# Where the routed experts' second layer and read-outs stand around eight runtime switches

## The chip, the cores and the metric

The kernel runs on one core of a Trainium2 chip. The metric is the device time of one execution in microseconds. The engines are PE (TensorE, matrix products), ACT (ScalarE), DVE (VectorE), POOL (GpSimd) and SP (SyncE, which issues most of the transfers). Each runs its own list of instructions in order, and they meet through semaphores. Where a branch depends on data, every engine takes it for itself.

## The reference

Three stages follow one another: a retention attention, a dense layer with a rational activation, and a mixture of experts. The change lies in the third:

```python
logits = x @ w_gate + modality_bias[modality_id]
e_idx = np.argmax(logits, axis=1)
...
for e in range(E):                       # 8 experts
    mask = e_idx == e
    if not mask.any():
        continue
    h = np.maximum(x[mask] @ w1[e], 0.0)         # 512 -> 1024
    out[mask] = gate_w[mask, None] * (h @ w2[e]) # 1024 -> 512
```

There are 3072 tokens. How many go to an expert is known only when the kernel runs.

## The kernel before

Values are split into a high and a low float16 part, and each product is made of three matmuls. Tokens are first written, sorted by expert, to a buffer `xs` in memory. Then the experts follow one another, `e` = 0 to 7.

Each expert has a static part of 288 columns (tokens) and an extra part of n columns, n = 0, 32, ..., 224. The static part is in the program as it stands. The extra part lies in one of the eight arms of a `tc.Switch` (L867), and each engine jumps to the arm that the count selects. `switch_hint` (L847) tells each engine the arm ahead of the jump, once the count has been loaded (`values_load`, L830). With these inputs the arms taken are n = 0, 128, 128, 192, 32, 64, 160 and 192 for the eight experts. A last `tc.If(redo > 0)` (L885) holds the path for an expert with more than 512 tokens; it is not taken here.

- `hidden` (matmuls L504) makes 128 of the 1024 hidden values of the columns: 12 matmuls, then a relu on ACT (L525, L535) and the low part on POOL or DVE (L537). Eight such steps, f0 to f7, make the layer; their results are `ht`. For extra columns `hidden_tile` does the same (`hq`, `hf`, `hx`).
- `combine` is the second layer: for the 288 columns, two tiles of 128 rows (L592) and one of 32 rows (L599), in three PSUM banks `acc0`, `acc1`, `acc2`, tile by tile within each f. Extra columns use `acc3`, `m`, `r`.
- `emit` is the read-out of a tile: for 128 rows a scale on DVE (L607), for the small ones a copy on ACT (L609), three additions (L611) and a scale (L612) on DVE; then an indirect transfer to `out`, issued by POOL (L613).
- Weights come in 512 KB pieces into five staging buffers (L439, L443 on SP), and `digest` splits each on ACT (L455) and DVE (L456). An expert has eight pieces. `weights()` fetches ahead and digests one; calls of it (`cfill`) stand between the steps of the layers.

The order is written out by hand: each engine does things in the order of the code. Expert 0 and 1 have an early part: the first 192 columns of expert 0's hidden layer and all 288 of expert 1's are made before the counts are known. Then stand the count (L772), two digests, and the loop. For each e: the count is read, the hint given, the hidden steps made that are left (`hd`; for e of 2 and above f3 to f7, since f0 to f2 stand in the arm before), with the read-outs of the expert before among them (the list `late`), then the static second layer, then the switch. An arm holds the extra hidden columns, the steps f0 to f2 of the next expert, and the extra second layer with its read-outs. The last expert has its static second layer and read-outs inside the arms, between its extra hidden columns and their second layer.

Of the kernel before, what the change touches and what calls it, by code (L numbers as in the profile page):

```python
# [54 lines left out]
def retention_moe_kernel(ctx, tc, qkv, qk, kv, w_in, w_out, ma, mb, mod, wg, mbias, w1, w2, consts, ids, out, dbg=None):  # L55
# [451 lines left out]
    def cut(n):  # L507
        tiles = [(t * P, P) for t in range(n // P)]
        for m in (64, 32):
            if n & m:  # L510
                tiles.append((sum(t[1] for t in tiles), m))
        return tiles
# [59 lines left out]
            ht.append(h)  # L572
        return lambda f: ht[f // m][:, f % m]

    def combine(nm, v2, ht, n, tags, fillers=(), serial=False):
        fillers = list(fillers)
        tiles = cut(n)
        spots = {}
        for a, b, h, l in places(n):
            for lo in range(a, b, P):  # L580
                spots[lo] = lo + h - a, lo + l - a
        ac = [ps.tile([P, DM], F32, tag=tag, name=f"ya{nm}_{lo}", bufs=1) for tag, (lo, _) in zip(tags, tiles)]
# [196 lines left out]
    def early(e, f):  # L779
        hidden(e, f, wts[e, 0], xge, 0, EARLY[e], "he", col[e], dve if (e, f) > (1, 0) else pool)  # L780
# [23 lines left out]
    early(0, 7)  # L804
    rank1()
    early(1, 0)
    mt, xg = load_rows("0", xs[:512], 512, EARLY[0])
    mtn, xgn = load_rows("1", xs[REG : REG + 512], 512, EARLY[1])
    for f in range(1, KF2):
# [13 lines left out]
    )  # L823
    dve.tensor_reduce(cnx[:, :E], over, axis=AX.X, op=ALU.add)
    dve.tensor_copy(cni[:, 2 * E + 1 :], cnx[:, :E])
    weights(2)

    def grains(e):
        at = 2 * E + 1 + e
# [3 lines left out]
        return nc.values_load(cni[0:1, e : e + 1], min_val=-NTOK if e == 2 * E else 0, max_val=NTOK)  # L833

    late = []

    for e in range(E):
# [8 lines left out]
        sel = grains(e)  # L846
        tc.switch_hint({g: sel for g in mybir.ALL_ENGINES}, nthr + 1, label=f"x{e}")  # L847
        lo = EARLY[e] if e < 2 else 0
        for f in range(FILL if e > 1 else 0, KF2):
            if lo < BASE:  # L850
                hidden(e, f, wts[e, 0], xg, lo, BASE, "hd")
            if late:
                late.pop(0)()
            if e > 1 and f in HFILL:
                cfill()
        def whole(nm):
            ac = combine(nm, wts[e, 1], lambda f, e=e: hts[e, f][:, 0], BASE, ("acc0", "acc1", "acc2"), [cfill if f < CFILL[min(e, 2)] else lambda: None for f in range(KF2)])
            return [lambda e=e, mt=mt, a=a, lo=lo, n=n: emit(e, nm, a, mt, SLOT[lo][1], n) for a, (lo, n) in ac]

        if last:  # L860
            redo = count(2 * E)
        else:
            late.extend(whole(e))
            if e:
                for f in range(FILL):
                    hidden_home(e + 1, f)
        for n in tc.Switch(sel, nthr + 1, hint=f"x{e}"):  # L867
            nm = f"{e}x{n}"
            n *= GRAIN
            if n:  # L870
                ht = hidden_tile(nm, wts[e, 0], xg, BASE, n, dve)
            if last:
                for f in whole(f"{e}b{n}"):
                    f()
            elif e:
                for f in range(FILL):
                    hidden(e + 1, f, wts[e + 1, 0], xgn, 0, BASE, f"hd{n}f", wide=False)
            if n:
                ac = combine(nm, wts[e, 1], ht, n, ("acc3", "m", "r"), serial=last)
                for a, (lo, m) in reversed(ac):  # L880
                    emit(e, nm, a, mt, SLOT[BASE + lo][1], m)
        if not last:
            mt, xg = mtn, xgn

    with tc.If(redo > 0):  # L885
        for e in range(E):
            cnt, start = count(e), count(E + e)
            with tc.If(cnt > start):
# [92 lines left out]
```

## Time and profile before

| | |
|---|---|
| median of 3 runs | 1014.28 us (1014.16 to 1014.75) |
| the profiled execution: its time | 1011.81 us |
| the profiled execution: its span | 1010.0 us |
| PE busy | 920.8 us, 91% of the span |
| DVE, ACT, POOL busy | 658.2, 603.7, 527.9 us |
| DMA, mean over the span | 119 GB/s |

The span is the part of the profiled execution in which engines worked. The experts take the stretch from about 660 us to the end. The timeline gives an instruction group's start and duration and, in brackets, how long its engine had been idle before it and what ended that. The waits sum this idle time by what ended it. `PEldq`, `POOLq` and the like are the engines' sequencers, which take branches and semaphores.

### The profile page before, as it was taken

To read this page: it belongs to the slowest core of one execution; us is meant where nothing else is said; L and a number is where in the kernel's file an instruction comes from. 1 tells how busy PE (TensorE), PEld (TensorE's weight loads), DVE (VectorE), ACT (ScalarE), POOL (GpSimd) and SP (SyncE) were. 2 spreads that over 40 slices of the span, in tenths; PEclk is the share of its full clock that TensorE was granted. 3 is DMA by queue.
4 is the path that set the end of the run, shared out by engine and by line. 5 is a ranking of instruction groups with operands and counts; after the bars stand their busy time and mean duration, and the time that the engine had idled before them with its cause. 6 is when DMAs were issued, how large, how long until landed. Compare 5 with 4: busy or idle time off the path is not lost.

```text
span 1010.0 us, 16225 instructions
## 1 busy us (share of the span) xinstructions
PE 920.8 (91%) x5957; PEld 503.0 (50%) x5957; DVE 658.2 (65%) x973; ACT 603.7 (60%) x964; POOL 527.9 (52%) x519
## 2 busy tenths in 40 slices
PE   8877889999999999989999999997799999999973
PEld 6534445444555445545444444455355664555641
DVE  4798777787888788877686797875426244553221
ACT  0376656877777677766776886874335454554320
POOL 2687878646666646666545545542315334344221
PEclk8779989999999999999999999998899999999987
DMA  8654877252214121410051033225665554672001
GB/s 280 197 208 143 262 223 251 86 153 93 67 63 126 73 77 61 105 43 1 1 146 43 1 80 105 85 63 164 173 203 162 171 163 146 178 209 60 15 26 43
DMA packets 105786, 119.93 MB, mean 119 GB/s; under 512 B 72030, under 2 KB 72286, under 8 KB 105568
## 3 DMA queue, kind: packets, MB, share of 16 engines
q1 hardware_dynamic: 101504, 104.98, 34.8%
q0 software_dynamic: 4064, 12.64, 3.5%
q8 instruction: 65, 1.06, 0.5%
q14 instruction: 153, 1.25, 0.4%
HBM read 81.83 MB, written 21.35 MB: 102 GB/s over the span
## 4 chain that ended last, share of the span: by engine, by line
PE 48%; DVE 17%; DMA 10%; issue 9%; POOL 8%; ACT 6%; SPq 0%; POOLq 0%; ACTq 0%; DVEq 0%; another core or an unknown queue 0%
PE hp L299 13%; PE acc L351 13%; PE ya L592 6%; DMA out<-yo2x,mt 5%; DMA out<-yo,mt 4%; PE y L231 2%; POOL q L310 2%; POOL xs L418 2%; PE sc L212 2%; PE y L229 2%; DVE q L321 2%; DVE r L320 2%; DVE q L319 2%; DVE p L312 1%; POOL gt L340 1%
## 5 line engine op out<-in xcount | busy, mean ns | idle before, releaser
L351 PE MATMUL acc<-woh,gt 128*128 128x512 f16 x768 | 245.3, 381 | 0.3 <-POOL gt L340 0.3
L299 PE MATMUL hp<-xt,wih 128*128 128x512 f16 x768 | 232.5, 385 | 1.1 <-DVE p L313 1.0
L310 POOL TENSOR_TENSOR q<-q,a 128x512 f32<-128x512 f32 x96 | 133.7, 1393 | 183.5 <-ACT q L309 183.2
L351 PEld LDWEIGHTS <-gt 128*128 128x128 f16 x1152 | 110.4, 98 | 127.7 <-issue 4.0
L299 PE MATMUL hp<-xt,wil 128*128 128x512 f16 x384 | 147.1, 383 | 0.0
L351 PE MATMUL acc<-wol,gt 128*128 128x512 f16 x384 | 146.3, 381 | 0.0
L504 PEld LDWEIGHTS <-we 128*128 128x128 f16 x1536 | 119.3, 100 | 36.7 <-issue 18.6
L319 DVE SCALAR_TENSOR_TENSOR q<-q,r 128x512 f32<-128x512 f32 x96 | 65.6, 683 | 95.7 <-ACT r L327 95.4
L299 PEld LDWEIGHTS <-wih 128*128 128x128 f16 x768 | 74.0, 99 | 91.4 <-issue 7.4
L340 POOL TENSOR_TENSOR gt<-q,gt 128x512 f16<-128x512 f32 x95 | 111.3, 1172 | 0.0
L326 ACT ACTIVATE r<-q,one 128x512 f32<-128x512 f32 x96 | 65.7, 684 | 66.9 <-POOL q L310 66.9
L456 DVE SCALAR_TENSOR_TENSOR we<-sw,we 128x1024 f16<-128x1024 f32 x64 | 83.3, 1332 | 31.0 <-ACT we L455 30.8
L307 ACT ACTIVATE p<-hp,co 128x512 f32<-128x512 f32 x96 | 74.3, 774 | 29.2 <-PE hp L299 28.9
L592 PE MATMUL ya<-we,ht 128*128 128x512 f16 x336 | 82.1, 396 | 10.1 <-DVE we L456 7.3
L309 ACT ACTIVATE q<-a,co 128x512 f32<-128x512 f32 x96 | 78.1, 814 | 12.1 <-POOL gt L340 3.4
L312 DVE TENSOR_TENSOR p<-p,hp 128x512 f32<-128x512 f32 x96 | 65.2, 679 | 14.9 <-ACT a L308 14.9
L455 ACT ACTIVATE we<-sw 128x1024 f16<-128x1024 f32 x64 | 64.9, 1042 | 16.9 <-DMA sw<-in_w 16.8
L313 DVE SCALAR_TENSOR_TENSOR p<-p,co,hp 128x512 f32<-128x512 f32 x96 | 71.6, 746 | 2.9
L320 DVE SCALAR_TENSOR_TENSOR r<-p,co,r 128x512 f32<-128x512 f32 x96 | 71.7, 747 | 0.0
L537 POOL TENSOR_TENSOR ht<-hfhd,ht 128x256 f16<-128x256 f32 (+1 forms) x76 | 51.3, 706 | 38.9 <-ACT ht L535 20.9
L339 ACT ACTIVATE gt<-q 128x512 f16<-128x512 f32 x96 | 59.9, 624 | 15.8 <-DVE q L321 11.2
L321 DVE SCALAR_TENSOR_TENSOR q<-q,r 128x512 f32<-128x512 f32 x96 | 65.9, 687 | 3.3
(232 smaller groups left out, 1392.2 us busy)
## 6 DMA issues: line engine op xcount, KB each, us to landing
sw<-in_w SPq DMA_DIRECT2D x64, 512.0 KB, 4.6
qk<-in_qk SPq DMA_DIRECT2D x22, 512.0 KB, 3.5
xs<-zrow SPq DMA_DIRECT2D x8, 1032.0 KB, 8.9
spare<-in_moe_w_in SPq DMA_DIRECT2D x8, 1024.0 KB, 6.2
spare<-in_moe_w_out SPq DMA_DIRECT2D x8, 1024.0 KB, 5.0
qk<-in_qkv SPq DMA_DIRECT2D x13, 512.0 KB, 4.9
kv<-in_qkv SPq DMA_DIRECT2D x13, 512.0 KB, 6.1
kv<-in_kv SPq DMA_DIRECT2D x11, 512.0 KB, 4.7
```

The lines of the kernel that those rows point to most:

```text
L299: pe.matmul(hp, wi[wj][:, k, f * P : (f + 1) * P], xt[:, xj, k], start=n == 0, stop=n == 3 * KD - 1)
L309: act.activation(q, a, AF.Identity, scale=b1, bias=b0)
L310: pool.tensor_tensor(q, q, a, op=ALU.mult)
L312: lambda: dve.tensor_tensor(p_, p_, hp, op=ALU.mult),
L319: lambda: dve.scalar_tensor_tensor(q, q, 1.0 + 1e-6, r, op0=ALU.add, op1=ALU.mult),
L320: lambda: dve.scalar_tensor_tensor(r, p_, n0, r, op0=ALU.add, op1=ALU.mult),
L321: lambda: dve.scalar_tensor_tensor(q, q, 2.0, r, op0=ALU.subtract, op1=ALU.mult),
L340: (dve if i == NS - 1 else pool).tensor_tensor(gt[:, 1], g, gt[:, 0], op=ALU.subtract)
L351: pe.matmul(accs[s], gt[:, gj, s * P : (s + 1) * P], wo[wj][:, f], start=f == 0 and gj == 0 and wj == 0, stop=f == NF - 1 and gj == 1)
L456: dve.scalar_tensor_tensor(dl, sv, sc, dh, op0=ALU.mult, op1=ALU.subtract)
L504: pe.matmul(hp, v1[:, wj, k, f * P : (f + 1) * P], xg[:, xj, k, cols], start=c == 0, stop=c == 3 * KD - 1)
L592: pe.matmul(a, ht(f)[:, at : at + P], v2[:, wj, f], start=first and at == h and wj == 0, stop=last and at == l)
```

## The change

1. One more weight piece is fetched after the first early step of expert 1, and one digest instead of two stands after the count.
2. Expert 0: the first tile of its static second layer (columns 0 to 127) is made ahead of the hint and of the hidden steps that are left. The other two tiles go into the switch's arms; three digests and the three read-outs follow the switch.
3. Expert 1 takes the banks `acc3`, `m`, `r` for its static tiles and `acc2`, `acc0`, `acc1` for the extra ones.
4. The static read-outs of experts 1 to 6 move from the next expert's hidden steps into the arms of their own switch, one behind each of the three hidden steps there.
5. Last expert: the hidden steps f5 to f7 move into the arms, behind the extra hidden columns; the extra second layer and its read-outs stay in the arm, and the static second layer comes after the switch, tile by tile from the last (32 rows) to the first.
6. The overflow path is given `preferred_fallthrough_block=False`: its empty block now stands first, and the body behind it.

```diff
+    def combine(nm, v2, ht, n, tags, fillers=(), serial=False, pick=slice(None), ac=None):
...
+        tiles = cut(n)[pick]
...
     early(1, 0)
+    prefetch()
     mt, xg = load_rows("0", xs[:512], 512, EARLY[0])
...
-    weights(2)
+    weights()
...
+        tags = ("acc3", "m", "r") if e == 1 else ("acc0", "acc1", "acc2")
+        xtags = ("acc2", "acc0", "acc1") if e == 1 else ("acc3", "m", "r")
...
+        out0 = []
+        if e == 0:
+            out0 = base("0a", pick=slice(0, 1))
+        announce()
+        if e != 1:
+            lo = EARLY[e] if e == 0 else 0
+            for f in range(FILL if e else 0, KF2 - FILL if last else KF2):
                 hidden(e, f, wts[e, 0], xg, lo, BASE, "hd")
-            if late:
-                late.pop(0)()
...
         if last:
             redo = count(2 * E)
+            inner = [(e, f, wts[e, 0], xg) for f in range(KF2 - FILL, KF2)]
+        elif e:
+            out0 = base(e, fill=CFILL[min(e, 2)])
+            inner = [(e + 1, f, wts[e + 1, 0], xgn) for f in range(FILL)]
...
+        for n in tc.Switch(sel[e], nthr + 1, hint=f"x{e}"):
...
+            outs = list(out0)
             if n:
                 ht = hidden_tile(nm, wts[e, 0], xg, BASE, n, dve)
+            if e == 0:
+                late[:] = out0 + base(f"0b{n}", pick=slice(1, 3), ac=ac0)
+            for k in inner:
+                hidden(*k, 0, BASE, f"hd{n}f", wide=False)
+                if e and outs:
+                    outs.pop(0)()
             if n:
-                ac = combine(nm, wts[e, 1], ht, n, ("acc3", "m", "r"), serial=last)
+                ac = combine(nm, wts[e, 1], ht, n, xtags)
...
+        if e == 0:
+            weights(3)
+            for f in late:
+                f()
+        if last:
+            for f in reversed(base(e, serial=True)):
+                f()
...
-    with tc.If(redo > 0):
+    with tc.If(redo > 0, preferred_fallthrough_block=False):
```

Where the instructions stand: three places. Names carry the expert and the tile: `ya0_128` is expert 0's static tile from column 128, `hd0_0` its hidden step f0, `yo2x4_3` a read-out of expert 2's arm 4. `cni` holds the counts.

PE from the count to the first products of expert 1, before (the last early step is just ahead of it):

```order
L772 MATMUL cntp_6680<-cum24_6487,ones_356 128x8 [waits Activation_49]
L830 TENSOR_LOAD cni_5784 [waits DVE_49]
...
L847 BRANCH_PREFETCH_HINT
L504 LDWEIGHTS we0_0_5375
L504 MATMUL hd0_0_6755<-xg0_6523,we0_0_5375 128x96 [waits DMAHW3_49]
...
L599 MATMUL ya0_256_6901<-we0_1_6230,ht0_7_6482 32x512
...
L867 BRANCH_PREFETCH_HINT
L977 UNCONDITIONAL_BRANCH [waits PE_49]
...
L830 TENSOR_LOAD cni_5784
...
L592 LDWEIGHTS ht1_0_6517
L592 MATMUL ya1_0_8188<-we1_1_6694,ht1_0_6517 128x512 [waits DVE_49]
```

After:

```order
L773 MATMUL cntp_6680<-cum24_6487,ones_356 128x8 [waits Activation_49]
L593 LDWEIGHTS ht0_0_6246
L593 MATMUL ya0a_0_6697<-we0_1_6230,ht0_0_6246 128x512
...
L593 MATMUL ya0a_0_6697<-we0_1_6230,ht0_7_6482 128x512
L832 TENSOR_LOAD cni_5784 [waits DVE_49]
...
L858 BRANCH_PREFETCH_HINT
L504 LDWEIGHTS we0_0_5375
L504 MATMUL hd0_0_6776<-xg0_6525,we0_0_5375 128x96 [waits DMAHW4_49]
...
L882 BRANCH_PREFETCH_HINT
L593 LDWEIGHTS ht0_0_6246
L593 MATMUL ya0_1_6920<-we0_1_6230,ht0_0_6246 128x512
```

The count's load, and with it the hint, has moved behind the 24 matmuls of `ya0a`. The arm's entry hint now stands between the hidden steps and the tiles `ya0_1` and `ya0_2`, which are in every arm.

DVE at the switch of expert 2, arm 4 (128 extra columns, the one taken), before:

```order
L537 TENSOR_TENSOR hx2x4_10766<-hf2x4_1_10869,hx2x4_10766 128x4x128 [waits Activation_49]
L607 TENSOR_SCALAR yo2x4_3_10952<-ya2x4_0_10927,mt2_8108 128x512 [waits DMASW7_49,DMASW3_49,PE_49]
L977 UNCONDITIONAL_BRANCH
...
L830 TENSOR_LOAD cni_5784
...
L847 BRANCH_PREFETCH_HINT
L607 TENSOR_SCALAR yo2_0_11761<-ya2_0_10032,mt2_8108 128x512 [waits DMASW3_49,DVE_49,PE_49]
L456 SCALAR_TENSOR_TENSOR we4_0_10092<-sw4_1_10064,we4_0_10092 128x1024 [waits DMAHW7_49,Activation_49]
L607 TENSOR_SCALAR yo2_1_11789<-ya2_128_10033,mt2_8108 128x512 [waits DMASW1_49,DMASW5_49,DVE_49,PE_49]
L456 SCALAR_TENSOR_TENSOR we4_0_10092<-sw4_2_10080,we4_0_10092 128x1024 [waits DMAHW0_49,Activation_49]
L611 TENSOR_TENSOR yo2_2_11817<-yo2_2_11817,ya2_256_10034 32x512 [waits DMASW2_49,DMASW6_49,PE_49,Activation_49]
```

After, the whole of the arm (its first two rows are the low parts of the extra hidden columns):

```order
L537 TENSOR_TENSOR hx2x4_11246<-hf2x4_0_11296,hx2x4_11246 128x4x128 [waits DMASW5_49,PE_49,DMASW6_49,Activation_49,DMASW7_49,Pool_49]
L537 TENSOR_TENSOR hx2x4_11246<-hf2x4_1_11349,hx2x4_11246 128x4x128 [waits Activation_49]
L608 TENSOR_SCALAR yo2_0_11371<-ya2_0_10437,mt2_8398 128x512 [waits DMASW1_49,DMASW5_49,DVE_49,PE_49]
L608 TENSOR_SCALAR yo2_1_11394<-ya2_128_10438,mt2_8398 128x512 [waits DMASW0_49,PE_49]
L612 TENSOR_TENSOR yo2_2_11417<-yo2_2_11417,ya2_256_10439 32x512 [waits DMASW3_49,DMASW7_49,PE_49,Activation_49]
L612 TENSOR_TENSOR yo2_2_11417<-yo2_2_11417,ya2_256_10439 32x512 [waits DVE_49] x2
L613 TENSOR_SCALAR yo2_2_11417<-yo2_2_11417,mt2_8398 32x512 [waits DVE_49]
L608 TENSOR_SCALAR yo2x4_3_11451<-ya2x4_0_11426,mt2_8398 128x512 [waits DMASW6_49,DMASW2_49,PE_49]
L1001 UNCONDITIONAL_BRANCH
L882 BRANCH_PREFETCH_HINT
```

The five rows that read `ya2` (one of them is two instructions) have moved from behind the next expert's hint into the arm, ahead of the read-out of the extra tile.

POOL from the end of the last switch's arm 6 (192 extra columns) to the end of the program, before:

```order
L613 DMA out_0<-yo7x6_5_20700,mt7_17201 3072x512 [waits DMAHW3_49,DMASW5_49,DVE_49]
L613 DMA out_0<-yo7x6_3_20707,mt7_17201 3072x512 [waits DMAHW1_49,DMASW6_49,DVE_49]
L867 ISA [waits DMASW7_49]
L977 UNCONDITIONAL_BRANCH
...
L885 COMPARE_AND_BRANCH
...
L885 ISA [waits Pool_49,Pool_sequencer_49,DMASW4_49,DMASW5_49,DMASW3_49,DMASW6_49,DMASW2_49,DMASW7_49,DMASW1_49,DMASW0_49]
L885 UNCONDITIONAL_BRANCH
L977 ISA [waits barrier_Pool_Activation_PE_DVE_SP_gather]
```

After:

```order
L614 DMA out_0<-yo7x6_5_21500,mt7_18157 3072x512 [waits DMAHW1_49,DMASW2_49,DVE_49]
L614 DMA out_0<-yo7x6_3_21507,mt7_18157 3072x512 [waits DMAHW7_49,DMASW3_49,DVE_49]
L882 ISA [waits DMASW4_49]
L1001 UNCONDITIONAL_BRANCH
...
L614 DMA out_0<-yo7_2_21842,mt7_18157 3072x512 [waits DMAHW6_49,DMASW5_49,DVE_49]
L614 DMA out_0<-yo7_1_21851,mt7_18157 3072x512 [waits DMASW6_49,DVE_49]
L614 DMA out_0<-yo7_0_21856,mt7_18157 3072x512 [waits DMASW7_49,DVE_49]
L909 COMPARE_AND_BRANCH
L909 ISA [waits Pool_49,Pool_sequencer_49,DMASW4_49,DMASW5_49,DMASW3_49,DMASW6_49,DMASW2_49,DMASW7_49,DMASW1_49,DMASW0_49]
L909 UNCONDITIONAL_BRANCH
```

The last transfers are now the three static ones behind the arm. The overflow test is followed at once by its empty block (the row with the many semaphores), and a jump then passes the overflow path.

## Rows read from the trace of the kernel before

**Rows 1.** Windows: PE, PEld, DVE, ACT, POOL busy us (x instructions), PEclk, DMA, GB/s.

```profile
695.00:745.00 50.00, 35.68 (x228) 17.57 (x225) 20.37 (x32) 17.20 (x32) 10.31 (x19) 0.83 0.67 195
745.00:945.00 200.00, 189.23 (x1560) 117.27 (x1557) 85.44 (x105) 94.21 (x166) 80.59 (x107) 0.99 0.51 148
945.00:994.00 49.00, 41.88 (x278) 24.24 (x276) 14.91 (x27) 10.59 (x22) 13.08 (x19) 0.93 0.11 36
```

**Rows 2.** The waits of PE, 690 to 1010 us.

```profile
PE ya L592 <- DVE we L456: 7.3, 1, 7.3
PE ya L599 <- DVE yo L611: 6.4, 4, 2.8
PE hq7x L504 <- ACT hf7x L525: 5.7, 1, 5.7
PE ya L592 <- DVE yo L607: 2.8, 3, 1.4
```

**Rows 3.** Timeline of PE, 695 to 745 us: start, us, line, tiles, [idle <-releaser].

```profile
699.38 3.11 PE L504 MATMUL hd<-xg,we 128*128 128x96 f16 x48 [3.37 <-DVE we L456]
719.39 2.76 PE L592 MATMUL ya<-we,ht 128*128 128x512 f16 x12
730.17 4.91 PE L592 MATMUL ya<-we,ht 128*128 128x512 f16 x12 [7.35 <-DVE we L456]
745.11 5.09 PE L504 MATMUL hq1x<-xg,we 128*128 128x128 f16 x88
```

**Rows 4.** Branches of PE, ns: L977 (720 to 731; 745 to 990 us) and L885.

```profile
L977 PEldq COMPARE_BRANCH  x2: 440/3244/6048, 719.7 to 723.1; - x2
...
L977 PEldq COMPARE_BRANCH  x13: 294/329/792, 756.2 to 990.0; - x13
...
L885 PEldq COMPARE_BRANCH  x1: 4879/4879/4879, 990.4 to 990.4; - x1
```

**Rows 5.** Timeline of SP and ACT, 720 to 740 us.

```profile
720.96 3.94 SPq L489 DMA_TRANSPOSE xg<-xs  x1
729.83 2.51 SPq L443 DMA_DIRECT2D sw<-in_w  x3
...
738.34 1.06 ACT L455 ACTIVATE we<-sw 128x1024 f16<-128x1024 f32 x1 [0.26 <-DMA sw<-in_w]
```

**Rows 6.** Timeline of PE in experts 3 and 4.

```profile
808.81 4.45 PE L592 MATMUL ya<-we,ht 128*128 128x512 f16 x12
842.83 7.51 PE L504 MATMUL hd<-xg,we 128*128 128x288 f16 x60 [1.50 <-DVE yo3x L611]
```

**Rows 7.** Timeline of the last expert, and the same product in expert 3.

```profile
820.26 8.09 PE L504 MATMUL hq3x<-xg,we 128*128 128x192 f16 x96
...
957.01 4.12 PE L504 MATMUL hq7x<-xg,we 128*128 128x192 f16 x48
972.37 0.81 PE L592 MATMUL ya7b<-we,ht 128*128 128x512 f16 x3
...
957.29 0.86 POOL L537 TENSOR_TENSOR ht<-hfhd,ht 128x256 f16<-128x256 f32 x2 [3.33 <-PE hd L504]
966.34 0.49 ACT L525 ACTIVATE hf7x<-hq7x 128x384 f32<-128x384 f32 x1 [2.93 <-issue]
```

**Rows 8.** The end: timeline of POOL, its landing, and the lines L885 and L977.

```profile
995.07 0.99 POOL L613 DMA_INDIRECT out<-yo7x,mt  x1 [3.27 <-DVE yo7x L607]
...
out<-yo7x,mt POOLq DMA_INDIRECT x2, 3.3
...
L885 POOLq COMPARE_BRANCH  x1: 62/62/62, 999.2 to 999.2; - x1
L885 POOLq INC_SWDGE_SEM  x1: 1324/1324/1324, 1003.0 to 1003.0; - x1
...
L977 POOLq COMPARE_BRANCH  x1: 45/45/45, 996.2 to 996.2; - x1
L977 POOLq DRAIN  x3: 40/109/4817, 1004.4 to 1009.8; - x3
```

More of the change, by code (lines that the diff above doesn't have):

```diff
@@ L573, in hidden_tile @@
         return lambda f: ht[f // m][:, f % m]
-    def combine(nm, v2, ht, n, tags, fillers=(), serial=False):
+    def combine(nm, v2, ht, n, tags, fillers=(), serial=False, pick=slice(None), ac=None):
         fillers = list(fillers)
-        tiles = cut(n)
+        tiles = cut(n)[pick]
         spots = {}
@@ L581, in combine @@
                 spots[lo] = lo + h - a, lo + l - a
-        ac = [ps.tile([P, DM], F32, tag=tag, name=f"ya{nm}_{lo}", bufs=1) for tag, (lo, _) in zip(tags, tiles)]
+        tags = tags[pick]
+        ac = ac or [ps.tile([P, DM], F32, tag=tag, name=f"ya{nm}_{lo}", bufs=1) for tag, (lo, _) in zip(tags, tiles)]
         steps = [(f, t) for f in range(KF2) for t in range(len(tiles))]
@@ L835, in retention_moe_kernel @@
     late = []
+    sel = {}
     for e in range(E):
@@ L844, in cfill @@
                 weights()
[L846 to L850, printed above, removed]
-                hidden(e, f, wts[e, 0], xg, lo, BASE, "hd")
-            if late:
-                late.pop(0)()
[L854 to L858, printed above, removed]
+        tags = ("acc3", "m", "r") if e == 1 else ("acc0", "acc1", "acc2")
@@ new lines, in retention_moe_kernel, with base, announce @@
+        xtags = ("acc2", "acc0", "acc1") if e == 1 else ("acc3", "m", "r")
+        def base(nm, tags=tags, fill=0, **kw):
+            ac = combine(nm, wts[e, 1], lambda f, e=e: hts[e, f][:, 0], BASE, tags, [cfill if f < fill else lambda: None for f in range(KF2)], **kw)
+            return [lambda e=e, mt=mt, a=a, lo=lo, n=n: emit(e, nm, a, mt, SLOT[lo][1], n) for a, (lo, n) in ac]
+        def announce():
+            sel[e] = grains(e)
+            tc.switch_hint({g: sel[e] for g in mybir.ALL_ENGINES}, nthr + 1, label=f"x{e}")
@@ L860, in retention_moe_kernel @@
+        out0 = []
[5 more added lines that the diff above has]
+            for f in range(FILL if e else 0, KF2 - FILL if last else KF2):
+                hidden(e, f, wts[e, 0], xg, lo, BASE, "hd")
+                if e and f in HFILL:
+                    cfill()
         if last:
             redo = count(2 * E)
-        else:
[L863 to L866, printed above, removed]
@@ L867, in retention_moe_kernel @@
-        for n in tc.Switch(sel, nthr + 1, hint=f"x{e}"):
+            inner = [(e, f, wts[e, 0], xg) for f in range(KF2 - FILL, KF2)]
+        elif e:
+            out0 = base(e, fill=CFILL[min(e, 2)])
+            inner = [(e + 1, f, wts[e + 1, 0], xgn) for f in range(FILL)]
+        else:
+            inner = []
+            ac0 = [ps.tile([P, DM], F32, tag=f"acc{t}", name=f"ya0_{t}", bufs=1) for t in (1, 2)]
+        for k in inner:
+            hidden_home(*k[:2])
+        banks = ["acc0", "acc1"] if e == 1 else ["m", "r"]
@@ L868, in retention_moe_kernel @@
+        for n in tc.Switch(sel[e], nthr + 1, hint=f"x{e}"):
             nm = f"{e}x{n}"
             n *= GRAIN
+            outs = list(out0)
             if n:
                 ht = hidden_tile(nm, wts[e, 0], xg, BASE, n, dve)
[L872 to L877, printed above, removed]
+            if e == 0:
+                late[:] = out0 + base(f"0b{n}", pick=slice(1, 3), ac=ac0)
+            for k in inner:
+                hidden(*k, 0, BASE, f"hd{n}f", wide=False)
+                if e and outs:
+                    outs.pop(0)()
@@ L878, in retention_moe_kernel @@
             if n:
-                ac = combine(nm, wts[e, 1], ht, n, ("acc3", "m", "r"), serial=last)
+                ac = combine(nm, wts[e, 1], ht, n, xtags)
                 for a, (lo, m) in reversed(ac):
                     emit(e, nm, a, mt, SLOT[BASE + lo][1], m)
-        if not last:
+        banks = ["m", "r"]
+        if e == 0:
[5 more added lines that the diff above has]
+                f()
+        else:
```

## The prediction

> **What bounds the kernel now.** The windows were read first, since the change touches only the last 315 us. PE is the busiest engine in each of them, but unevenly. From 745 to 945 us, experts 1 to 6, it is busy for 189.23 of 200 us at a clock of 0.99; at the start of the experts, 695 to 745, for 35.68 of 50 at 0.83; in the last expert, 945 to 994, for 41.88 of 49 at 0.93 (the figure before the DMA share) [rows 1]. So PE's waits set the time, and what they hold can be won without making anything faster. The waits of PE come next: the largest is 7.3 us, then 6.4 and 2.8 for read-outs of `ya`, then 5.7 in the last expert [rows 2]. The third view, the timeline, says where they stand, and corrects one name. The 7.3 us are put down to DVE's `we`, but PE's last product before them ended at 730.17 - 7.35 = 722.82, and its sequencer spent 6.05 us of the gap in one branch, that at the end of expert 0's empty arm; the 13 later ones take 0.29 to 0.79 us [rows 3, 4]. That wait is a jump, not data.
>
> The sum is made against the profiled execution, 1011.81 us; the median of the runs, 1014.28, is 2.5 above it, which is added at the end.
>
> **Part (a), experts 0 and 1 (points 1 to 3 of the change).** In the trace the extra columns of expert 1 (`hq1x`) start at 745.11 [rows 3]. Until then PE has, after the count, at 699.38 - 3.37 = 696.0, a wait of 3.37 for the counts, 96 small matmuls of `hd`, and the two static second layers. The second one takes 745.11 - 730.17 = 14.94, of which 4.91 - 2.76 = 2.15 is a first group at the lower clock, so 12.8 at full clock [rows 3].
>
> After the change PE goes from the count at once to tile 0a: 24 matmuls, twice the 2.76 of a group of 12, about 5.4 us, to 701.4. That covers the wait for the counts, which ended at 699.38. The 96 matmuls of `hd` at 3.11 for 48 are at most 6.2 [rows 3]: 707.6. Tiles 0b are the rest of a static layer, 12.8 - 5.4 = 7.4: 715.0. Expert 1's static layer no longer waits for expert 0's read-outs, having other banks, and adds 12.8: 727.8. By PE alone `hq1x` is 17.3 us earlier.
>
> Something else is late next: ACT. Its digests wait for weights, and these for SP, which after expert 0's switch first loads rows of expert 2 (it starts at 720.96 and gets to the next weights at 729.83, 8.9 us), so that the third digest behind it ran at 738.34 to 739.40 [rows 5]. All this hangs on SP's passage through the switch and comes forward with it. I estimate by 5 us, since SP needs one digest ahead of the loads, that the change puts later in ACT's order. Then ACT ends its digests at 734.4, pays about 2.9 at the arm's entry (its stall at the last expert's [rows 7]) and 2.6 for two relus of the extra part (two instructions each, by the 0.49 for 384 columns [rows 7]), and relus the step f0 at about 740. PE, with two banks for these steps, needs that for f2, after `hq1x` (5.09 for 88 of 96 matmuls [rows 3], so 5.6) and two steps of 1.5: 727.8 + 5.6 + 3.0 = 736.4. PE waits about 3.5, and 14 of the 17.3 are left. **(a) = -14**, bounds -19 (digests early) and -8 (both of PE's branches around expert 0's arm at 6.05, and ACT's wait).
>
> **Part (b), read-outs in the arms (point 4).** What goes is the wait of the next static layer for banks that are still being read: 6.4 us in four waits (small tile) and 2.8 in three (128-row tiles) [rows 2]. After the longest of them, 2.76 at expert 3, the next group took 4.45 for 2.76, 1.7 us at the lower clock [rows 3, 6]. Together 10.9. In the arm the read-outs stand behind f0, f1 and f2, so that the banks are free before the extra second layer begins. What is added there: POOL has per step 0.86 for the low part and 0.99 for the transfer's issue [rows 7, 8], 1.85, while PE makes a step in 7.51 / 5 = 1.5 us [rows 6]. POOL falls back by 0.35 a step, 1.1 in three, and ACT, whose relu needs a buffer that POOL frees, with it. The extra second layer is the cover. It is thin where there are 32 extra columns, and there 1 us may show. The 1.50 at expert 4 (a bank of the extra read-out) [rows 6] stays. **(b) = -9.5**, bounds -11 and -4 (each of the six arms giving back 1.1).
>
> **Part (c), last expert (point 5).** From `hq7x` at 957.01 to the static layer at 972.37 PE took 15.4 us for work that took 8.09 in expert 3: 7.3 lost, 5.74 of it in the wait for ACT [rows 2, 7]. ACT was late because POOL was: its low parts began only at 957.29, after expert 6's arm, and ACT then stalled 2.93 at the branch [rows 7]. After the change the static read-outs of expert 6 are no longer between these low parts, ACT reaches the branch two or three steps sooner, and f5 to f7 stand behind `hq7x` as cover. But POOL still leaves expert 6's arm late, and `hq7x`'s relu needs the buffers of f3 and f4, which POOL frees at 957.3 + 0.9 = 958.2 at the soonest, while PE, with f5 to f7 (4.5 us) behind it instead of ahead, starts `hq7x` at 952.5 and has the half that fits two banks done 4.12 later, at 956.6 [rows 7]. With the relu's 0.5 that leaves a wait of about 2.1. **(c) = -5**, bounds -7 and -2.
>
> **Part (d), the end (points 5 and 6).** POOL issued the last transfer at 995.07, which landed 3.3 us later, at about 998.4. Meanwhile it passed the arm's exit (996.2) and got to the overflow test at 999.2, 3.0 us later; that test jumped, and the counter step followed at 1003.0 and the drain at 1004.4 [rows 8]. After the change no arm's exit stands behind the last transfer, and the test falls through. POOL is ready for the counter step when the transfer has landed, some 0.5 later: 998.9, and 1.4 on is 1000.3. Then comes the jump over the overflow path. Priced like the old test's (999.2 to 1002.5, by the 1003.0 less 0.5) it costs 3.2, and the drain begins at 1003.5 instead of 1004.4. **(d) = -1**, bounds -4.1 (this jump is free) and +0.5 (it costs PE's 4.88 [rows 4]).
>
> The digests that come two pieces later are costed at nothing: PE at 0.99 and ACT at 94.21 of 200 us in the middle window [rows 1] leave them room. If that cover is gone, it is the slower rival below.
>
> Sum: -14 - 9.5 - 5 - 1 = -29.5. 1011.8 - 29.5 = 982.3 profiled, 1014.3 - 29.5 = 984.8, **985 us**, for the median.
>
> **A rule against the change.** The row on branches shows one long jump out of a short arm and short ones elsewhere [rows 4]. The Trainium skill, page "Runtime: NRT & Kernel Launch", section "Instruction fetch mechanics", says that a taken branch whose target lies outside the window of pages that the engine holds must fetch the page before it goes on. By this rule expert 0's entry and exit would both pay, as would the jump over the overflow path. The trace agrees for the one exit and for the test's 4.88, not for the 13 jumps in between. By the rule the sum would be that of the first rival, by the 13 rows that of the forecast.
>
> **The rivals.**
> - PE pays for its code around expert 0's arm. The counts are there at 699.4, and the hint with them; before, the entry followed 20 us later, at 719.7, and cost 0.44, and the exit 3.4 us behind the entry cost 6.05 [rows 3, 4]. Now the entry follows some 5 to 7 us behind the counts and the exit some 8 behind the entry, between the two. At 6.05 each, with 0.8 us of small matmuls queued ahead of the entry and 3.3 of large ones ahead of the exit, PE loses 5.2 + 2.7 = 7.9. `hq1x` starts at 735.7 and ACT's wait vanishes in it: (a) is -9.4, the time 989 (984.8 + 4.6).
> - The waits only move: POOL and ACT fall back in the arms, and the steps after them wait for relus. For it: POOL's 1.85 against 1.5 a step. Against it: POOL is busy for 80.59 of 200 us [rows 1]. (b) shrinks to -3.5, (c) to -2: 994.
> - The best case: the digests come early, the last jump is free. (a) -18, (d) -4: 978.
> - Slower: the weights. The digests stand two pieces later, and SP can fetch only when a digest has freed a staging buffer. If the static layers of experts 2 to 7 each waited for their last piece, six waits would undo 29.5 us from 29.5 / 6 = 4.9 us each; at 5.5 the time is 1018. For it: DMA is busy for 0.67 in the early window. Against it: it is 0.51 in the middle one [rows 1], and no wait of PE there is for `we`, the 7.3 having been the jump [rows 2].
> - The overflow test doesn't do what it says, and the empty block still pays a jump like the old one: that is already in (d).
>
> **How the numbers follow.** The forecast, 981 to 988.5, gets 0.55; PE's code 0.15 (989); moved waits 0.15 (994); the best case 0.08 (978); the weights 0.05 (1018); nothing gained, 1014, 0.02. Low and high take in the forecast's bounds, the code, the best case and most of the moved waits: 976 to 995. A measurement of this kernel tells about 0.2% (2 us) from no change. Faster by more: 0.55 + 0.15 + 0.15 + 0.08 = 0.93; within it 0.02; slower 0.05.
>
> **What would show it.** (a): `hq1x` starts at 728 to 732 in the changed trace, with a wait of PE for ACT's relu in expert 1's arm of 2 to 5 us; a branch of PE over 3 us at 704 to 720 speaks for the code rival. (b): no waits of PE for `yo` in experts 2 to 6 except that on an extra bank, 1.5 us. (c): `hq7x` with a wait of 2 us instead of 5.7 and no half at the lower clock. (d): 8.4 us from the last transfer's issue to the drain's start, where it was 1004.4 - 995.1 = 9.3, and the counter step right behind the landing. The prediction is wrong if PE waits for `we` in the experts, or if waits of ACT for POOL in the arms reach PE.

## The result and the profile after

The changed kernel takes 997.84 us (median of 4 runs, 996.74 to 998.69), against 1014.51 for the kernel before on the same chip: a ratio of 0.9828, interval 0.9805 to 0.9851. That is 16.7 us faster; the forecast was 29.5 faster, 985, and the range ended at 995. The direction held, the size didn't.

The profiled execution took 997.75 us with a span of 995.9. Up to the count (L772, in the changed kernel L773) the two kernels differ by one weight fetch alone (point 1), but in the two profiles the count came at 695.84 and 698.57 us. In three profiles of the changed kernel it came between 695.70 and 698.94: what stands ahead of it varies by a few us from execution to execution. So times below are counted from the start of the count's matmul.

| stretch (by the starts of TensorE's groups) | before | after | difference | forecast |
|---|---|---|---|---|
| count to expert 1's extra columns (`hq1x`) | 49.3 | 31.3 | -18.0 | -17.3 |
| from there to expert 2's step f3 | 15.0 | 25.3 | +10.3 | +3.5 |
| to expert 7's step f3 | 188.1 | 184.3 | -3.8 | -9.5 |
| to TensorE's end | 45.9 | 42.4 | -3.4 | -5 |
| to the span's end | 16.0 | 14.0 | -2.0 | -1 |
| sum | 314.2 | 297.4 | -16.8 | -29.3 |

The waits of PE from 690 us on, which answer to [rows 2] (line, tile, releaser: us in total, times, longest):

```profile
PE hd128f L504 <- ACT hfhd128f L525: 7.9, 1, 7.9
PE hq7x L504 <- issue: 3.0, 1, 3.0
PE hq4x L504 <- issue: 2.9, 1, 2.9
PE hd L504 <- DVE yo L613: 2.6, 1, 2.6
PE ya L593 <- DVE we L456: 1.5, 1, 1.5
```

Of [rows 2] only the first label is left, with 1.5 us instead of 7.3 (the jump behind expert 0's arm); the waits of the static layers for `yo` and the wait of `hq7x` for ACT are gone. In their place stand 7.9 us for ACT in expert 1's arm (`hd128f`), 2.9 and 3.0 at the entries of the arms of experts 4 and 7 ("issue": nothing that the profile shows was waited for), 2.6 for a read-out behind expert 4's arm, and smaller ones.

The windows, with the columns of [rows 1]:

```profile
698.00:748.00 50.00, 39.45 (x349) 22.26 (x349) 19.43 (x32) 19.03 (x36) 7.29 (x20) 0.95 0.64 164
748.00:940.00 192.00, 183.41 (x1454) 111.01 (x1453) 89.66 (x111) 92.86 (x163) 74.39 (x110) 0.99 0.57 163
940.00:982.00 42.00, 37.56 (x257) 23.02 (x255) 10.90 (x22) 9.73 (x21) 9.99 (x16) 0.96 0.09 28
```

The clock and PE's share rose at the start (39.45 of 50 at 0.95, where it was 35.68 at 0.83) and in the last expert (37.56 of 42 at 0.96). In the middle PE is busy for 183.41 of 192, 8.6 us idle, hardly less than the 10.8 of 200 before.

The start of `hq1x` and the step that then waits, in the timeline of PE:

```profile
729.86 5.53 PE L504 MATMUL hq1x<-xg,we 128*128 128x128 f16 x96
...
747.12 3.03 PE L504 MATMUL hd128f<-xg,we 128*128 128x288 f16 x12 [7.87 <-ACT hfhd128f L525]
```

By PE alone the first stretch came as worked out. What then made it wait 7.87 us is in the timelines of DVE, SP and ACT of the same time, with the landing time of expert 0's first read-out between them:

```profile
718.67 0.74 DVE L608 TENSOR_SCALAR yo0a<-ya0a,mt 128x512 f32<-128x512 f32 x1
728.31 0.75 DVE L608 TENSOR_SCALAR yo0b<-ya,mt 128x512 f32<-128x512 f32 x1 [8.90 <-DMA out<-yo0a,mt]
...
732.79 5.77 DVE L456 SCALAR_TENSOR_TENSOR we<-sw,we 128x1024 f16<-128x1024 f32 x5 [1.21 <-ACT we L455]
...
DMA to landing us min/median/max: 8.5/8.5/8.5
...
716.93 6.86 SPq L489 DMA_TRANSPOSE xg<-xs  x1
...
727.99 8.69 SPq L443 DMA_DIRECT2D sw<-in_w  x4
...
731.38 1.06 ACT L455 ACTIVATE we<-sw 128x1024 f16<-128x1024 f32 x1 [9.59 <-DMA sw<-in_w]
...
737.83 1.06 ACT L455 ACTIVATE we<-sw 128x1024 f16<-128x1024 f32 x1 [2.43 <-DMA sw<-in_w]
744.36 0.60 ACT L525 ACTIVATE hf1x<-hq1x 128x512 f32<-128x512 f32 x1 [5.47 <-issue]
```

Read from the top. DVE scaled the first read-out at 718.67 and could not begin the second until 728.31: 8.90 us, by the releaser for the landing of the first one's transfer, which took 8.5 us. Behind the read-outs in DVE's order stand its halves of the digests, five in a row from 732.79. Until these are made no staging buffer is free, and SP's four weight fetches took from 727.99 to 736.7. ACT, which has its own halves of six digests ahead of the arm, waited for each piece and ended the last at 738.89. Then 5.47 us passed at the arm's entry. ACT's sequencer had taken the branch into the arm at 738.0, and the arm's first instruction came 6.1 us later. At the same entry before the change it was 3.4 us, which cost nothing there, since `hq1x` came later still:

```profile
L1001 ACTq COMPARE_BRANCH  x1: 43/43/43, 738.0 to 738.0; - x1
...
L882 ACTq BRANCH_PREFETCH_HINT  x1: 36/36/36, 744.1 to 744.1; - x1
...
L977 ACTq COMPARE_BRANCH  x1: 43/43/43, 738.5 to 738.5; - x1
...
L867 ACTq BRANCH_PREFETCH_HINT  x1: 36/36/36, 742.0 to 742.0; - x1
```

The first relu of the arm ran at 744.36, 45.8 from the count, where the forecast had 737.3 - 695.8 = 41.5.

The branches of PE at the entry and exit of expert 0's arm and at the entries of the arms of experts 4 and 7, and the hints ahead of the last two (ns; start in us), as in [rows 4]:

```profile
L1001 PEldq COMPARE_BRANCH  x2: 357/2082/3807, 707.4 to 712.1; - x2
...
L1001 PEldq COMPARE_BRANCH  x1: 5624/5624/5624, 850.4 to 850.4; - x1
...
L1001 PEldq COMPARE_BRANCH  x1: 3703/3703/3703, 943.2 to 943.2; - x1
...
L858 PEldq BRANCH_PREFETCH_HINT  x1: 40/40/40, 829.0 to 829.0; - x1
...
L858 PEldq BRANCH_PREFETCH_HINT  x1: 35/35/35, 937.3 to 937.3; - x1
```

And what stands around them: PE, then DVE behind expert 4's arm, then PE in the last expert:

```profile
856.28 2.75 PE L504 MATMUL hq4x<-xg,we 128*128 128x32 f16 x96 [2.90 <-issue]
...
868.00 2.24 PE L504 MATMUL hd<-xg,we 128*128 128x288 f16 x17 [2.63 <-DVE yo L613]
...
867.38 0.47 DVE L613 TENSOR_SCALAR yo<-yo,mt 32x512 f32<-32x512 f32 x1
...
947.08 9.74 PE L504 MATMUL hq7x<-xg,we 128*128 128x192 f16 x96 [2.96 <-issue]
```

At expert 4 the hint had been given 21.4 us ahead and the branch still took 5.62. At expert 7 it had been given 5.9 us ahead and took 3.70. At expert 0, where it had been given 5.4 us ahead (701.96), the branch took 0.36. So the lead alone doesn't decide. Behind expert 4's arm PE waited until DVE had scaled the small static tile (867.38 + 0.47 = 867.85): its copy on ACT stands behind the third step's relu, and the extra second layer, which was to cover it, is 1.8 us long with 32 columns.

The end, as in [rows 8]: POOL's last transfer, its branches at the overflow test, the counter step and the drain:

```profile
982.97 0.99 POOL L614 DMA_INDIRECT out<-yo,mt  x1 [2.90 <-POOLq L909]
...
L909 POOLq COMPARE_BRANCH  x2: 42/49/56, 982.7 to 987.6; - x2
L909 POOLq INC_SWDGE_SEM  x1: 1328/1328/1328, 986.3 to 986.3; - x1
...
L1001 POOLq DRAIN  x3: 44/109/4883, 990.2 to 995.6; - x3
```

The test no longer jumps, but the empty block ends in a jump (the second branch, 987.6), behind which the drain starts at 990.2.

### The profile page after: what moved, and what is told of

Same layout as the page of the kernel before. It is cut to its first block, busy times and chain, and to the rows that moved or that the text cites. A ratio compares the mean times of both kernels' runs of the same rounds, so it can differ in the third digit from the quotient of the medians.

```text
span 995.9 us, 16233 instructions
## 1 busy us (share of the span) xinstructions
PE 917.2 (92%) x5957; PEld 501.6 (50%) x5957; DVE 661.0 (66%) x973; ACT 603.7 (61%) x964; POOL 515.8 (52%) x519
## 5 line engine op out<-in xcount | busy, mean ns | idle before, releaser
L504 PEld LDWEIGHTS <-we 128*128 128x128 f16 x1536 | 117.3, 99 | 44.2 <-issue 24.4
L537 POOL TENSOR_TENSOR ht<-hfhd,ht 128x256 f16<-128x256 f32 (+1 forms) x70 | 41.4, 616 | 46.7 <-ACT ht L535 21.7
```

Of the source, the lines that this page charges most:

```text
L504: pe.matmul(hp, v1[:, wj, k, f * P : (f + 1) * P], xg[:, xj, k, cols], start=c == 0, stop=c == 3 * KD - 1)
```

## The experiments

All kernels but the last two are the changed kernel with one edit or none. Single profiles are compared from the count on. The runs of one kernel lie 2 to 9 us apart, and the intervals of the ratios reach 2 to 6 us to each side.

**The changed kernel again, twice.** No edit.

> The changed kernel once more, for its second profile. Theory (a long branch hangs on where the code lies): TensorE's branch into expert 4's arm takes 5 to 6 us again, and that into the last arm 3 to 4. Rival (a branch is long by chance, as the transfers happen to lie): the 5.6 us are at another branch or nowhere. Time 997.8 +- 1.5 by both.

> The changed kernel a third time, beside the two above on the same chip: 996 to 999, from the count to the end 295 to 297.5; the branch into expert 4's arm 5 to 6 us as in its other profiles.

Medians 997.58 and 998.47 us; from the count to the end 295.1 and 296.9. The wait of PE for ACT in expert 1's arm (7.9, 7.8, 7.4 us in the three profiles) and the long branch into expert 4's arm (5.62, 6.23, 6.12 us; its gap 2.9, 3.3, 3.2) are properties of the program, not of one execution. The stretch of the last expert is less firm: 42.4, 40.4 and 42.2. The difference lies in `hq7x`, which took 9.74, 8.09 and 9.74: from 946 to 957 us the mean granted clock was 0.84 in the first profile, part of it at the lower level, and 1.00 in the second.

**Buffers of their own for expert 0's read-outs.**

```diff
-        o = mp.tile([P, DM], F32, tag="t1", name=f"yo{nm}_{s}", bufs=4)[:n]
+        own = e == 0 and str(nm).startswith("0b") and s in (1, 2)
+        o = ep.tile(..., tag=f"z{s}", bufs=1)[:n] if own else mp.tile(..., tag="t1", bufs=4)[:n]
```

> Expert 0's second and third static read-outs get buffers of their own, so that DVE doesn't wait 8.9 us for the landing of the first one. Theory (this wait holds up DVE's digests, these the staging buffers and SP, these ACT's digests and with them ACT's entry into expert 1's arm): ACT's last digest ahead of the arm ends 3.5 to 4.5 us earlier against the count, TensorE's wait of 7.9 us in the arm falls to 3 to 5, time 993 to 995. Rival (ACT is late because SP's loads of expert 2's rows stand before the weights): DVE's wait goes, ACT's last digest moves by less than 1 us, time 997 to 998.

Median 991.63 us (ratio to before 0.9769, 0.9734 to 0.9805), somewhat below the time expected. The wait of PE, DVE's read-outs, ACT's last digest ahead of the arm:

```profile
PE hd128f L504 <- ACT hfhd128f L525: 3.6, 1, 3.6
...
716.55 0.75 DVE L609 TENSOR_SCALAR yo0a<-ya0a,mt 128x512 f32<-128x512 f32 x1
717.21 0.74 DVE L609 TENSOR_SCALAR yo0b<-ya,mt 128x512 f32<-128x512 f32 x1
...
733.34 1.06 ACT L455 ACTIVATE we<-sw 128x1024 f16<-128x1024 f32 x1 [1.04 <-DMA sw<-in_w]
```

The second read-out follows the first at once, and PE's wait is 3.6, the 3.5 of the forecast. ACT's last digest ends at 734.40, 37.6 from the count instead of 40.3, somewhat less than expected; another 2.0 us came at the arm's entry, whose stall was 3.5 instead of 5.5 (why is open). From the count to the end 291.0, 4 to 6 less than in the changed kernel's three profiles. The theory holds: the false link was DVE's wait for a buffer. In the changed kernel's profile the second read-out waits for the landing of the first one's transfer. The ring of four buffers had been handed round the arms (twelve read-outs in all, in the order of the code), and the former user of that buffer is a read-out in an arm that isn't taken. That the count waited for can then only be reached by the next transfer on that queue is argued from this, not tried by itself.

**Fewer digests ahead of expert 1's arm.**

```diff
-CFILL = (4, 6, 5)
+CFILL = (4, 4, 5)
```

> Expert 1's static layer has 4 digests among its steps instead of 6; the two come later. Theory (TensorE's wait in expert 1's arm is ACT's, which must pass six digests and their weights before it may enter the arm): the last two, at 734.3 and 737.8 us, no longer stand ahead of the arm, ACT enters some 6 us earlier, the 7.9 us fall to 1 to 3, time 991 to 994. Rival (the weights come too late anyway, and the wait only moves to the next static layer): the 7.9 us fall but a wait for digested weights of 4 us or more appears in expert 2, time 996 to 998.

Median 991.23 us (ratio 0.9754, 0.9713 to 0.9794). PE's waits in the arms of experts 2 and 3, and ACT in expert 3's arm:

```profile
770.45 1.63 PE L504 MATMUL hd128f<-xg,we 128*128 128x288 f16 x12 [1.55 <-ACT hfhd128f L525]
...
805.97 6.64 PE L504 MATMUL hq3x<-xg,we 128*128 128x192 f16 x48 [4.41 <-ACT hf3x L525]
...
805.42 0.49 ACT L525 ACTIVATE hf3x<-hq3x 128x384 f32<-128x384 f32 x1 [5.17 <-issue]
```

Theory and rival were both partly right. In expert 1's arm PE no longer waits for ACT at all, and from the count to expert 2's step f3 it takes 45.5 us instead of 56.2 to 56.6, so ACT's way into the arm was the limit. But the weights that were put off come due in experts 2 and 3: ACT enters the arm late, stalls 5.17 in the second, and PE waits 1.55 and 4.41 for it. Behind the longer wait `hq3x` ran at the lower clock (a mean of 0.63 from 805.9 to 813; 6.64 us where its first half took 4.13). From expert 2's step f3 to expert 7's it takes 194.9 us instead of 184.3. So in this profile the gain was gone by the end (295.2 from the count); in the medians some of it stayed.

**The code of one arm made longer.**

```diff
+            if e == 3 and n == 224:
+                pad = ps.tile([P, DM], F32, tag="acc3", name="pad", bufs=1)
+                for _ in range(64):
+                    pe.matmul(pad, ht(0)[:, 0:P], wts[e, 1][:, 0, 0], start=True, stop=True)
```

> 64 more matmuls in the arm of expert 3 for 224 columns, which is not taken: nothing more is executed, but all of TensorE's code behind it lies 128 instructions further on. Theory (the branch of 5.6 us into expert 4's arm hangs on where hint, branch and target lie in the code): that branch takes under 1 us or another one of experts 4 to 7 becomes long; the ones before are as they were. Rival (it is the transfers of that moment): the branch still takes 5 to 6 us. Time 994 to 999.

The added matmuls stand in an arm that isn't taken. Median 993.40 us (ratio 0.9771, 0.9737 to 0.9806). The branch into expert 4's arm, and the wait of PE in expert 5's:

```profile
L1005 PEldq COMPARE_BRANCH  x1: 308/308/308, 851.8 to 851.8; - x1
...
PE hd64f L504 <- ACT hfhd64f L525: 2.6, 1, 2.6
```

The branch takes 0.31 us instead of 5.6 to 6.2, with the same hint 21.3 us ahead. So it was where the code lies that made it long. In this profile, of the slowest of the four runs, 2 of the 3 us were given back in expert 5 (2.6 in its arm and 1.1 behind it for ACT, 3.7 together, where the changed kernel's three profiles have 1.2 to 1.9), and from the count to the end it takes 295.6 us, where the changed kernel takes 295.1 to 297.4. The median is 4 to 5 us lower. In the last kernel below, with the same shift, the wait for ACT in and behind expert 5's arm is 0.8; why ACT is late there in one and not in the other stays open.

The Trainium skill, page "Runtime: NRT & Kernel Launch", section "Instruction fetch mechanics", says that a taken branch whose target lies outside the window of pages that the engine holds must fetch the target's page before it goes on. That the length of code that isn't executed decides over a branch of 5.6 us agrees with it; which pages are held at a branch no run here shows.

**The last expert's steps ahead of the switch.**

```diff
-            for f in range(FILL if e else 0, KF2 - FILL if last else KF2):
+            for f in range(FILL if e else 0, KF2):
...
-            inner = [(e, f, wts[e, 0], xg) for f in range(KF2 - FILL, KF2)]
+            inner = []
```

> The changed kernel with the last expert's hidden steps f5 to f7 ahead of the switch again, the rest as changed. Theory (TensorE's branch into the last arm costs 3.3 to 3.7 us because only two steps, 6 us, lie between hint and branch): with five steps the branch takes under 1 us, the wait of 2.6 to 3.0 us at the branch goes, but without f5 to f7 behind them the relus of the extra columns wait for POOL, 2 to 4 us; from hint to TensorE's end 41.5 to 43, as with the change (42.4). Rival (the branch is long whatever the lead): it stays at 3 us and the stretch gets longer, 44 or more.

Median 1001.33 us (ratio 0.9878, 0.9828 to 0.9927), 3 to 4 slower than the changed kernel, whose intervals overlap this one. The branch into the last arm, and PE's wait behind it:

```profile
L1001 PEldq COMPARE_BRANCH  x1: 399/399/399, 950.3 to 950.3; - x1
...
PE hq7x L504 <- ACT hf7x L525: 3.7, 1, 3.7
```

With five steps between hint and branch it takes 0.40 us, with two 3.1 to 3.8; and without f5 to f7 in the arm PE waits 3.7 for ACT. The stretch to PE's end is 44.1 us, longer than the theory had it, against 40.4 to 42.4 with the steps in the arm and 45.9 before. So part 5 is worth 1.7 to 3.7 by these steps. If the hint came earlier it might be worth some 3 more, an estimate from the gap of 2.6 to 3.0 at the branch that wasn't tried. The shorter arms also put this kernel's code elsewhere. Against that as the cause, the three other kernels here whose code was moved (the longer arm twice, the read-outs as before) kept 3.1 to 3.4 us at this branch. But expert 0's entry took 0.36 with a hint 5.4 us ahead, so what a lead is worth isn't settled.

**The overflow test as before.**

```diff
-    with tc.If(redo > 0, preferred_fallthrough_block=False):
+    with tc.If(redo > 0):
```

> The changed kernel without the out-of-line overflow block. Theory (the test's jump is only put behind the landing, and half of the 2.0 us between TensorE's end and the span's end come from the arm's exit, which no longer stands behind the last transfer): 14.5 to 15.5 us from TensorE's end to the span's end, against 14.0 with the change and 16.0 before. Rival (the block is all of it): 16.0.

One run, 992.66 us. POOL at the end:

```profile
980.67 0.99 POOL L614 DMA_INDIRECT out<-yo,mt  x1 [2.88 <-DVE yo L608]
...
L909 POOLq EVENT_SEMAPHORE  x6: 17/30/43, 983.3 to 983.8; - x6
...
L909 POOLq COMPARE_BRANCH  x1: 65/65/65, 980.4 to 980.4; - x1
L909 POOLq INC_SWDGE_SEM  x1: 1337/1337/1337, 983.8 to 983.8; - x1
...
L1001 POOLq DRAIN  x3: 40/109/4817, 985.2 to 990.6; - x3
```

Neither theory: from PE's end to the span's end it takes 11.3 us, with the out-of-line block 13.7 to 14.2 in nine profiles. (The last two kernels below, which have the plain test too, take 11.2 and 11.3.) POOL's sequencer reaches the test at 980.44, ahead of the last transfer (980.67), which still waits for DVE in POOL's queue. The jump's 2.8 us (to the first semaphore at 983.3) pass while the transfer is issued and lands, and the counter step begins at 983.84. From transfer to drain it is 985.2 - 980.67 = 4.5 us, against 7.2 with the block out of line and 9.3 before. So the gain at the end comes from part 5 alone, which took the arm's exit from behind the last transfer; part 6 costs 2.7 us.

**The small tile read first.**

```diff
-            outs = list(out0)
+            outs = list(reversed(out0))
```

> The changed kernel with the static read-outs in the arms in the order small tile, second, first. Theory (the 2.6 us that TensorE waits at the start of expert 5's steps are the small tile's copy, three additions and scale, which begin only behind the last of the three steps): they begin two steps, 3 us, earlier, and the wait falls to 0 to 1; the 1.5 and 1.4 us at experts 4 and 7, which are the extra read-outs, stay or fall by up to 1. Rival (DVE is late through the low parts and relus in the arm): it stays over 2.

Median 996.39 us (ratio 0.9852, 0.9807 to 0.9897), like the changed kernel. The waits of PE behind expert 4's arm and in expert 3's:

```profile
PE hq3x L504 <- ACT hf3x L525: 1.6, 1, 1.6
...
PE hd L504 <- DVE yo L608: 1.1, 1, 1.1
```

The 2.6 became 1.1, now for a 128-row tile, somewhat more than expected; the copy had been the cause. But 1.6 us for ACT appeared in expert 3's arm, where the changed kernel's three profiles have none, and nothing is left in the time.

**The read-outs of experts 2 to 5 as before.**

```diff
+                if 2 < e < E - 1 and late:
+                    late.pop(0)()
...
-            outs = list(out0)
+            outs = list(out0) if e < 2 or e > E - 3 else []
...
+        if 1 < e < E - 2:
+            late[:] = list(out0)
```

> The changed kernel with the static read-outs of experts 2 to 5 among the next expert's steps again, as before the change. Theory (moving them took away 0.4 to 2.8 us at each following static layer and gave back 2.6 and 1 to 1.5 us in the arms of experts 4 and 5): the waits of the small tile and the 128-row tiles are back, 7 to 9 us in all, the 2.6 is gone; from expert 3's first step ahead of the switch to expert 6's 3 to 6 us longer than with the change (109.8). Rival (the waits only moved): within 1 us.

Median 1003.75 us (ratio 0.9908, 0.9882 to 0.9934), 5 to 6 slower than the changed kernel. The waits of PE for read-outs:

```profile
PE ya L600 <- DVE yo L612: 3.9, 3, 1.6
PE ya L593 <- DVE yo L608: 3.7, 4, 1.1
```

They are back, 7.6 us in seven waits, and the 2.6 behind expert 4's arm is gone. By the stretch that was expected, from expert 3's step f3 to expert 6's, the rival was right: 109.4 us, against 108.9 to 110.5 in the changed kernel's three profiles. That stretch leaves out the last of the waits, in expert 6's static layer; to expert 6's extra columns it takes 133.5 us, against 130.5 to 131.1 with the change and 133.8 before. The shorter arms also put the code elsewhere: the branch into expert 4's arm took 2.0 us here and left no gap, where the changed kernel has 2.9 to 3.3. So by estimate the move itself is worth some 6 us in these experts, of which the long branch takes 3. The median's 5 to 6 us are not these: from the count to the end this profile takes 297.6, hardly more than the changed kernel's 295.1 to 297.4.

**What was found, put together.** Own buffers and the plain test; then the longer arm as well. Both edits are those above.

> Two findings put together: buffers of their own for expert 0's second and third read-out, and no out-of-line block. Theory (they stand at different places and add up): from the count to the end 291.0 less 2.8, 288; TensorE's wait in expert 1's arm 3 to 4 us, 11.2 us from TensorE's end to the span's end; time 987 to 990. Rival (the end of the program is late by something else once TensorE ends earlier): 14 us at the end, time 991.

> The same with 64 more matmuls in expert 3's arm for 224 columns, which isn't taken, so that the code behind it lies elsewhere. Theory (the branch into expert 4's arm then takes 0.3 us, but what it gives is mostly taken back by the relus in expert 5's arm, 2 to 3 us): from the count to the end 286 to 288, time 985 to 989. Rival (the 3 us are won in full): 284 to 285, time 983 to 985.

The first: median 991.32 us (ratio 0.9793, 0.9734 to 0.9851), 291.4 from the count to the end. Both were expected lower. The end is 11.2 us, as forecast. The exit of expert 0's arm took 5.3 us instead of 3.1 to 3.8, and PE waited 3.0 there, but its wait in expert 1's arm fell to 0.4, and up to expert 2's step f3 this profile takes 50.0 us, 2.2 less than with own buffers alone. What was lost lies behind: to expert 7's step f3 it takes 188.1 us, against 184.4 with own buffers alone, with 1.5 us for ACT in expert 3's arm and 2.9 in and behind expert 5's, where that kernel has none and 1.4; and the last expert takes 42.1 against 40.6. Why ACT was later there stays open.

The second: median 981.41 us (979.24 to 984.61; ratio 0.9686, 0.9639 to 0.9734), 16 to 17 faster than the changed kernel and the fastest of all. Its largest waits of PE, and the window of the middle:

```profile
PE hq7x L504 <- issue: 2.6, 1, 2.6
PE hd L504 <- DVE yo L614: 2.6, 1, 2.6
PE hd128f L504 <- ACT hfhd128f L525: 2.4, 1, 2.4
...
747.00:930.00 183.00, 176.71 (x1427) 107.46 (x1424) 88.14 (x108) 90.22 (x159) 68.17 (x101) 1.00 0.56 164
```

From the count to the end it takes 282.0 us, 11.3 of them behind PE's end: shorter than either expected. No wait at an entry is left but the last arm's, and in the middle PE is idle for 6.3 of 183 us. Against the changed kernel's three profiles, up to expert 2's step f3 it is 49.7 instead of 56.2 to 56.6 us, to expert 7's 180.6 instead of 184.3 to 184.9, behind PE's end 11.3 instead of 13.7 to 14.0. So this order of work can win what was forecast for it. That the three findings alone do it isn't shown: the two kernels differ only by code that isn't executed, and by 9.4 us from the count to the end, of which the branch into expert 4's arm is 3.2. The rest, such as the waits for ACT that are gone, was not tried by itself.

## Why the prediction was wrong

**Part (a), -14 forecast, -7.7 found.** The first half held: `hq1x` came 18.0 us earlier, forecast 17.3. The exit of expert 0's arm took 3.81 us and the entry 0.36; with the products queued ahead this left 1.5 us of wait, so the code rival was a small part. The step that failed is "comes forward with it. I estimate by 5 us": ACT's digests came forward by 3.2 against the count (739.40 - 695.84 = 43.6 before, 738.89 - 698.57 = 40.3 after), and the stall at the entry, taken at 2.9, was 5.5: 1.8 and 2.6, by which the wait was 4.4 longer. The estimate took SP's passage as the only thing behind the digests. SP did get to the weights 4.6 earlier (729.83 - 695.84 = 34.0 before, 727.99 - 698.57 = 29.4 after). But the second read-out of expert 0, which before the change followed the first in a row, had come to wait 8.9 us for a landing, with DVE's digests behind it, and these held up SP's further fetches. With own buffers the wait is the forecast's. The stall was taken from the last expert's arm. At this very entry ACT's branch had left 3.4 us before the change, and at the seven entries from expert 1 on it left 0.4 to 4.5 before and 2.2 to 6.1 after: the 2.9 was one value out of a wide range, and what sets it stays open. The lower clock behind the wait (a mean of 0.50 from 747.1 to 750) cost the step f2 another 1.4 (3.03 for 1.63), and PE waited 0.6 for digested weights there.

**Part (b), -9.5 forecast, -3.8 found.** The removal was right: all the waits in the 10.9 went. With the read-outs of experts 2 to 5 put back, 7.6 us of such waits are there again. What was given back was mis-sized: 2.6 us for the small tile's read-out behind the arm with 32 columns, which the prediction had named as the thin cover and priced at 1; 1.5 for ACT in and behind expert 5's arm, for which the prediction's lag of POOL and ACT is the likely cause, though no run tried it by itself; and 2.9 for the branch into expert 4's arm, which wasn't in it at all: 7.0 together, where 1.4 had been allowed. The prediction looked for a long branch at expert 0 alone, where the trace had shown one, and took the 13 short ones [rows 4] for a property of hinted branches. At expert 4's arm the longer arm showed it to be one of where the code lies, which the change moved everywhere.

**Part (c), -5 forecast, -3.4 found,** with 40.4 to 42.4 in three profiles about the size. The wait for ACT did go. The forecast's remaining 2.1 for POOL's buffers didn't show as such, since PE came later by 3.0: its branch, with only two steps behind the hint, took 3.7. That price of part 5 was left out. Nor did `hq7x` stay clear of the lower clock: it took 9.74 us, where it took 8.09 in the one of the three profiles that shows none there.

**Part (d), -1 forecast, -2.0 found.** The picture was right in that the jump is only put behind the landing; it took 2.6 instead of 3.2, and from the last transfer's issue to the drain it was 7.2 instead of 8.4. What was not seen is that the plain test would have been hidden: part 6 alone is a loss of 2.7.

**The rivals.** The moved waits, 994, came nearest, for the most part by other mechanisms than the one named: a buffer's wait and code that had moved, beside the lag of POOL and ACT. The weights rival didn't come: in the middle PE doesn't wait for `we`. The 1.5 us under that name at the start are the exit of expert 0's arm, as the 7.3 were, and the 0.6 in expert 1's arm are the only real ones.

## What to carry to other kernels

When read-outs are moved past other work, look at what each of them waits for, buffers of a ring included: a ring that is handed round arms can make a tile wait for the transfer of the one before it. A branch's price is not a constant to be read from the branches of another program: look for it again in the changed one, on every engine that takes the branch, and give the hint as early as the counts allow. Even code that isn't executed moved this kernel's time, by 4 to 10 us in the medians of two trials, so a small gain can be one of where the code lies. What an engine's sequencer reaches early, as a test that stands behind a queued transfer, is free until something makes it wait behind that transfer.

## What the runs showed of the hardware

- TensorE's branch into the same arm with the hint 21 us ahead took 5.6 to 6.2 us in the changed kernel's three profiles and 0.31 when code that isn't executed was made 64 matmuls longer.
- With the hint 5.9 us ahead the branch into the last arm took 3.70 us (3.1 to 3.8 in the kernels with two steps between), with five steps between 0.40. At expert 0's entry it took 0.36 with the hint 5.4 us ahead.
- ScalarE's branch into expert 1's arm is recorded with 0.04 us, but the arm's first instruction came 6.1 us later (3.4 before the change), although its hint had been given 21.7 us ahead (716.34). From the entry of expert 1's arm to that of expert 7's this gap was 0.4 to 4.5 us in the kernel before and 2.2 to 6.1 in the changed one.
- An indirect transfer to `out` landed 8.5 us after its issue while SP's loads of rows and weights were under way, and 3.3 us at the quiet end.
